# The transforms over D split nine by 64, with the nine points on VectorE

## The chip, the cores and the metric

The kernel runs on one core of a Trainium2 chip. The metric is the time on the device in microseconds (us), the median of the runs shown. Each core has a matrix engine (TensorE, PE in the profile), VectorE (DVE), ScalarE (ACT), GpSimd (POOL) and a queue engine for transfers (SyncE, SP), which run side by side and wait for one another through semaphores. Matmuls write to PSUM, which has eight banks per partition; the other engines evacuate PSUM to SBUF.

## The reference

The output is `g * a + (1 - g) * b`, for x of 2048 rows (S) and 576 columns (D):

```
X = rfft2(x);  X = X * (w_r + 1j * w_i);  a = irfft2(X, s=(S, D))
b = (gelu(x2 @ w_gate) * (x2 @ w_up)) @ w_down        # F = 4608
g = sigmoid((x * gate_w).sum(-1))
```

What is computed is the output and the gradients for all inputs but the second x (x2): for x, w_r, w_i, the three weight matrices and gate_w. So the spectral part needs the 2-D transform of x and of the gated gradient, their products with the filter and with one another (the gradient of the filter has the shape of the filter, 2048 by 289), and two inverse transforms: of the filtered spectrum and of the spectrum that gives the gradient for x.

## The kernel before, in words

The kernel has two phases. In the first, 18 groups g of 256 columns of F are taken with four blocks m of 512 rows each: 72 rows of work, each some 12 to 15 us long. In one of them TensorE does z (L466, L471: the gradient times w_down, transposed), xy (L475, L482: x2 times gate and up), and weight-gradient jobs of the group before: dwd (L595), dw (L613), and in the block m = 2 a tail dwt (L627). ScalarE evacuates xy and z (L494 to L504), computes sigmoids (L530 to L534), and VectorE does the products of GELU and its gradient (`H_ew1`, `H_ew2`; L509 to L551). The stores of weight gradients go out on POOL's queue (L605, L620, L631, L632).

The spectral work ("fft units") is fitted into these rows in slots. `want(pr)` says how many units are done by row pr, from the list `FIRST` for the first nine rows and from a linear share after it. The first slot of a row (`k0`) lies inside the second xy; the others lie between the weight-gradient jobs. All units and z share one PSUM tile of two banks: `pz` has one buffer, so the next z or unit waits until the evacuation of the unit before it.

The forward units work on 16 tiles t of 128 rows for x and 16 for the gradient. The transform over D = 576 is split as 6 residues r (column = 6 q + r) by 96: ScalarE first copies a row tile to `xq` with stride 6 (`sort`, L728; L730 with a scale for the gradient), `u1` multiplies each residue (a lhsT of 96 columns) with a table Rt over the rows (L657, six matmuls of 128 columns), evacuates to Z, and `u2` multiplies Z with the table F (L671, six of 98 columns). ScalarE evacuates to `ve` (L677) and VectorE combines the six points (L679 to L698) into the spectrum `Vt` in natural order of l = 0 to 288, which is stored to DRAM (`scr_x`, `scr_g`).

The middle units take p = 0 to 7, each with 16 of the rows g of the spectrum: `prefetch(p)` loads Vp and the filter Wt (twelve transfers on POOL, L770), `s2` (L779) finishes the transform over S in the units x0, x1, g0, g1 (evacuated at L784), `products` puts the products with the filter in a list `side`, which VectorE works off after `H_ew1`, and `s1` (L857) begins the inverse transforms in four units. The gradient of the filter, `o1`, is stored directly. `prefetch(0)` stands ahead of the middle units, `prefetch(1)` in the last x/g unit of p = 0, and `prefetch(p + 2)` in the second `s1` of p.

The second phase (from some 912 us) accumulates the two matmul results over F per tile of 128 rows (L1235) and, between them, finishes the inverse transforms over D: for each tile i and each w in (output, gradient) `fold` (VectorE, L1266 on) makes F from the spectrum, `z_piece` (L1287, six matmuls of 128 columns) and `d_piece` (L1297, six of 96) transform it, and ScalarE evacuates the six residues to `yo` with stride 6 (L1299). `x_out` (L1415) evacuates the accumulators; `post` mixes with the gate.

The order of the work is written out by hand; nothing reorders it later. Each engine runs its instructions in the order of the program.

Of the kernel before, what the change touches and what calls it, by code (L numbers as in the profile page):

```python
# [38 lines left out]
LQ = 49  # L39
SIN60 = math.sqrt(0.75)  # L40

# [20 lines left out]
def iotas(nc, res, unit):  # L62
    tb = Tables()
    G, V = nc.gpsimd, nc.vector
    kw = dict(allow_small_or_imprecise_dtypes=True)
    tb.halfpi = res.tile([P, 1], F32, name="halfpi")
    V.memset(tb.halfpi[:], math.pi / 2)
    tb.pi = res.tile([P, 1], F32, name="pi")
    V.memset(tb.pi[:], math.pi * EPS_SCALE)
    tb.warm = res.tile([P, 1], F32, name="warm")  # L70
    nc.scalar.activation(tb.warm[:], tb.halfpi[:], ACT.Sigmoid)
    tb.lrow = unit([LQ], F32, name="lrow")
    G.iota(tb.lrow[:], pattern=[[1, LQ]], base=0, channel_multiplier=0, **kw)
    tb.dcol = res.tile([P, 6], F32, name="dcol")
    for k, (r, step, n) in enumerate(((1, 1, 2), (0, 0, 1), (5, -1, 3))):
        k0 = (0, 2, 3)[k]
        G.iota(tb.dcol[:, k0:k0 + n], pattern=[[step, n]], base=r, channel_multiplier=6, **kw)
    tb.late = []
    tb.Rt = []
    return tb  # L80
# [39 lines left out]
def build_F(nc, tb, unit):  # L120

    V = nc.vector
    step = 2.0 * math.pi / D
    X = unit([6, LQ], F32, name="XF")
    y = unit([6, LQ], F32, name="yF")
    V.tensor_tensor(X[:], tb.dcol[:].unsqueeze(2).to_broadcast([P, 6, LQ]), tb.lrow[:].unsqueeze(1).to_broadcast([P, 6, LQ]), op=ALU.mult)
    V.tensor_scalar(y[:], X[:], 1.0 / D, MAGIC, op0=ALU.mult, op1=ALU.add)
    V.tensor_scalar(y[:], y[:], -MAGIC, -float(D), op0=ALU.add, op1=ALU.mult)
    V.tensor_tensor(X[:], X[:], y[:], op=ALU.add)
    V.scalar_tensor_tensor(y[:], X[:], -1.0, X[:], op0=ALU.mult, op1=ALU.max)  # L130
    tb.F = unit([6, 2, LQ], name="Ft")

    def sines():
        nc.scalar.activation(tb.F[:, :, 0], y[:], ACT.Sin, bias=tb.halfpi[:], scale=-step)
        nc.scalar.activation(tb.F[:, :, 1], X[:], ACT.Sin, scale=-step * EPS_SCALE)
    tb.late.append(sines)


def build_I(nc, tb, ftile, small, out):

    V = nc.vector
    R = slice(0, 2 * LQ)
    col = small([8])
    lp, ge, mul, add, e0, e1, half, q_ = (col[R, k:k + 1] for k in range(8))
    X, y = ftile()[R], ftile()[R]

# [5 lines left out]
    kw = dict(allow_small_or_imprecise_dtypes=True)  # L152
    nc.gpsimd.iota(q_, pattern=[[0, 1]], base=0, channel_multiplier=1, **kw)
    nc.gpsimd.iota(X.rearrange("p (r q) -> p r q", r=6), pattern=[[1, 6], [6, 96]], base=0, channel_multiplier=0, **kw)
    V.tensor_scalar(ge, q_, float(LQ), None, op0=ALU.is_ge)
    ts(lp, ge, -float(LQ), 0.0)
    tt(lp, lp, q_, ALU.add)
    ts(mul, ge, -2.0, 1.0)
    tt(mul, mul, lp, ALU.mult)
    ts(add, ge, -float(D // 4), float(D // 4))  # L160
    ts(X, X, mul, add)
    ts(y, X, 1.0 / D, MAGIC)
    ts(y, y, -MAGIC, -float(D), op0=ALU.add, op1=ALU.mult)
    tt(X, X, y, ALU.add)
    V.tensor_scalar(e0, lp, 0.0, None, op0=ALU.is_equal)
    V.tensor_scalar(e1, lp, float(LQ - 1), None, op0=ALU.is_equal)
    tt(half, e0, e1, ALU.add)
    ts(half, half, -0.5, 1.0)
    o = out[R].rearrange("p r q -> p (r q)")
    nc.scalar.activation(o, X, ACT.Sin, scale=2.0 * math.pi / D * EPS_SCALE)  # L170
    V.tensor_scalar(o, o, half, None, op0=ALU.mult)
# [120 lines left out]
def kernel(  # L292
# [355 lines left out]
    def fwd_units(src, dst, scale):  # L648
        zs = {}
        CLS = (1, 2, 0, 5, 4, 3)  # L650

        def u1(t):
            def f():
                zps = pftile()
                row = src.pop(t)
                for k, r in enumerate(CLS):
                    nc.tensor.matmul(zps[0:96, k // 3, k % 3 * P:(k % 3 + 1) * P], lhsT=row[:, r], rhs=tb.Rt[t], start=True, stop=True)  # L657
                zs[t] = unit([2, 3 * P], name="Z")
                if scale is None:
                    nc.scalar.copy(zs[t][0:96], zps[0:96, :, 0:3 * P])  # L660
                else:
                    nc.scalar.activation(zs[t][0:96], zps[0:96, :, 0:3 * P], ACT.Copy, scale=scale)
            return f

        def u2(t):
            def f():
                Z = zs.pop(t)
                vps = pftile()
                w = 2 * LQ
                for k in range(6):  # L670
                    nc.tensor.matmul(vps[:, k // 3, k % 3 * w:(k % 3 + 1) * w], lhsT=Z[0:96, k // 3, k % 3 * P:(k % 3 + 1) * P],  # L671
                                     rhs=tb.F[0:96, k].rearrange("p c l -> p (c l)"), start=True, stop=True)
                Vt = half([2, DF], name="Vt")
                ve = unit([2, 3, 2, LQ], F32, name="ve")
                sd = unit([2, 3, 2, LQ], F32, name="sd")
                M = unit([6, 2, LQ], F32, name="vm")
                nc.scalar.copy(ve[:].rearrange("p b k c l -> p b (k c l)"), vps[:, :, 0:3 * w])  # L677
                lo, hi = ve[:, 0], ve[:, 1]
                V.tensor_tensor(sd[:, 0], lo, hi, op=ALU.add)  # L679
                V.tensor_tensor(sd[:, 1, :, 0], hi[:, :, 0], lo[:, :, 0], op=ALU.subtract)  # L680
                V.tensor_tensor(sd[:, 1, :, 1], lo[:, :, 1], hi[:, :, 1], op=ALU.subtract)
                e, o = sd[:, 0, 2], sd[:, 1, 2]
                for k, op in enumerate((ALU.add, ALU.subtract)):
                    V.tensor_tensor(M[:, k], sd[:, 0, 0], sd[:, 0, 1], op=op)
                    V.tensor_tensor(M[:, 4 + k, 1::-1], sd[:, 1, 0], sd[:, 1, 1], op=op)
                p_, m_ = M[:, 0], M[:, 1]
                for c, op in enumerate((ALU.subtract, ALU.add)):
                    V.scalar_tensor_tensor(M[:, 2, c], m_[:, c], 0.5, o[:, c], op0=ALU.mult, op1=op)
                V.scalar_tensor_tensor(M[:, 3], p_, -0.5, e, op0=ALU.mult, op1=ALU.add)
                up = Vt[:, :, 96:DF - 1].rearrange("p c (j l) -> p j c l", j=2)[:, :, :, 0:LQ]  # L690
                dn = Vt[:, :, 1:193].rearrange("p c (j l) -> p j c l", j=2)[:, :, :, 94:47:-1]
                V.tensor_tensor(Vt[:, :, 0:LQ], e, p_, op=ALU.add)
                V.scalar_tensor_tensor(Vt[:, 0, DF - 1:DF - LQ:-1], o[:, 0, 0:LQ - 1], -1.0, m_[:, 0, 0:LQ - 1], op0=ALU.mult, op1=ALU.subtract)
                V.tensor_tensor(Vt[:, 1, DF - 1:DF - LQ:-1], m_[:, 1, 0:LQ - 1], o[:, 1, 0:LQ - 1], op=ALU.subtract)
                for c in range(2):
                    V.scalar_tensor_tensor(up[:, :, c], M[:, 4:6, c], SIN60, M[:, 2:4, c], op0=ALU.mult, op1=ALU.add)
                for c, s_, op in ((0, -SIN60, ALU.add), (1, SIN60, ALU.subtract)):
# [786 lines left out]
```

## Time and profile before

| | |
|---|---|
| Median of 3 runs | 1360.02 us (1359.3 to 1360.67) |
| The profiled execution | 1359.78 us, its span 1358.0 us |
| Granted TensorE clock | 1.0 |
| TensorE busy | 1343.7 us (99%) |
| VectorE busy | 879.8 us (65%) |
| ScalarE busy | 770.3 us (57%) |
| POOL busy | 243.9 us (18%) |
| Chain that ended last | PE 98% |

The span is the time from the first to the last instruction in the trace; some 1.8 us lie around it. Busy times of an engine add the times in which it works; its instructions overlap in their pipelines, so the time from start to start of two dependent instructions is shorter than the duration of one. The chain that ended last is followed back from the last instruction, at each step to what released it; a share of 98% says that nearly the whole span is TensorE at work, one matmul after another. In groups, "idle before" is the time that the engine stood idle just before these instructions, with what ended it.

### The profile page before, as it was taken

How to read it: one execution, taken by the hardware profiler on the slowest of the kernel's cores; microseconds unless marked ns; L12 is line 12 of the kernel's file. 1: busy time of each engine (PE TensorE's matmuls, PEld its weight loads, DVE VectorE, ACT ScalarE, POOL GpSimd, SP SyncE). 2: the span in 40 equal slices, each digit the busy share in tenths (PEclk: the TensorE clock that was granted, in tenths of full speed). 3: DMA queues.
4: the chain of work that ended last, by engine and by line, in shares of the span. 5: the costliest groups of instructions: out<-in, count | busy, mean ns of one | idle time of the engine just before them, and what ended most of it. 6: DMA issues, size and time to landing. Idle time of an engine off the chain costs nothing.

```text
span 1358.0 us, 26951 instructions
## 1 busy us (share of the span) xinstructions
PE 1343.7 (99%) x10279; PEld 900.6 (66%) x10360; DVE 879.8 (65%) x2353; ACT 770.3 (57%) x1380; POOL 243.9 (18%) x488
## 2 busy tenths in 40 slices
PE   9999999999999999999999999999999999999999
PEld 6556656656655655655655655568888888888887
DVE  7988898898857876876776855526543455354420
ACT  6797887888767776776777675622332232232210
POOL 3011111111313633434323311000000000000000
PEclk9999999999999999999999999999999999999999
DMA  9624435534543644644754658499999787888773
GB/s 224 181 73 125 137 100 150 155 99 132 152 138 108 180 119 119 168 123 118 175 141 116 159 127 181 116 240 237 201 205 213 162 175 160 167 163 175 155 154 75
DMA packets 493606, 207.05 MB, mean 152 GB/s; under 512 B 313346, under 2 KB 485444, under 8 KB 493476
## 3 DMA queue, kind: packets, MB, share of 16 engines
q1 hardware_dynamic: 467330, 170.47, 55.2%
q0 software_dynamic: 15040, 24.38, 6.4%
q10 hardware_dynamic: 11106, 10.48, 3.1%
q8 instruction: 81, 1.33, 0.4%
q14 instruction: 49, 0.40, 0.1%
HBM read 41.18 MB, written 89.11 MB: 96 GB/s over the span
## 4 chain that ended last, share of the span: by engine, by line
PE 98%; issue 1%; DMA 1%; SPq 0%; ACT 0%; DVE 0%
PE acc L1235 31%; PE wps L613 18%; PE xy L482 18%; PE wps L595 10%; PE z L466 9%; PE wps L627 2%; PE xy L475 2%; PE z L471 2%; PE pf L657 1%; PE acc L1287 1%; PE pf L671 1%; PE acc L1297 1%; PE pf L857 1%; PE pf L779 1%; DMA xn<-in_A_x_dram 1%
## 5 line engine op out<-in xcount | busy, mean ns | idle before, releaser
L1235 PEld LDWEIGHTS <-pin 128*128 128x128 bf16 x3456 | 334.9, 98 | 82.4
L482 PE MATMUL xy<-wgu,xT 128*128 128x512 bf16 x1082 | 257.6, 379 | 8.6 <-issue 7.3
L613 PE MATMUL wps<-dH,xn 128*128 128x512 bf16 x1141 | 263.7, 379 | 0.6
L613 PEld LDWEIGHTS <-xn 128*128 128x128 bf16 x1152 | 111.3, 98 | 125.4 <-issue 0.6
L482 PEld LDWEIGHTS <-xT 128*128 128x128 bf16 x1152 | 105.7, 98 | 132.9 <-issue 24.8
L595 PE MATMUL wps<-dB,A 128*128 128x288 bf16 x1152 | 149.9, 286 | 0.0
L620 POOL DMA_DIRECT2D out_dram<-dw x134 | 73.1, 549 | 423.5 <-ACT dw L564 411.7
L1235 PE MATMUL acc<-wgT,pin 128*128 128x288 bf16 x1152 | 146.5, 286 | 0.0
L1235 PE MATMUL acc<-wd_all,pin 128*128 128x288 bf16 x1152 | 146.4, 286 | 0.0
L1235 PE MATMUL acc<-wuT,pin 128*128 128x288 bf16 x1152 | 146.0, 286 | 0.0
L1299 ACT ACTIVATE yo<-acc 128x288 bf16<-128x288 f32 x64 | 67.4, 1246 | 132.1 <-PE acc L1297 120.7
L466 PE MATMUL z<-wdT,dOT 128*128 128x256 bf16 x1152 | 138.2, 273 | 0.1
L595 PEld LDWEIGHTS <-A 128*128 128x128 bf16 x1152 | 111.8, 98 | 32.9
L494 ACT ACTIVATE da<-z,omg 128x256 bf16<-128x256 f32 x288 | 111.9, 470 | 28.8 <-PE z L471 28.6
L466 PEld LDWEIGHTS <-dOT 128*128 128x128 bf16 x1152 | 112.0, 98 | 22.3 <-ACT dOT L438 0.5
L1415 DVE TENSOR_TENSOR b16t<-acc,f32t 128x288 bf16<-128x288 f32 x32 | 14.6, 457 | 168.4 <-PE acc L1235 168.3
L503 ACT CAST xb<-xy 128x512 bf16<-128x512 f32 x144 | 85.5, 594 | 39.5 <-PE xy L482 39.5
L1289 ACT CAST Z<-acc 98x384 bf16<-98x384 f32 x64 | 27.5, 481 | 112.8 <-PE acc L1287 112.8
L504 ACT CAST hu<-xy 128x512 bf16<-128x512 f32 x144 | 87.8, 610 | 0.0
L541 DVE TENSOR_TENSOR xb<-xb,sg 128x1024 bf16<-128x1024 bf16 x48 | 33.1, 689 | 81.2 <-ACT sg L533 81.2
L501 ACT ACTIVATE q<-xy 128x512 bf16<-128x512 f32 x144 | 80.6, 605 | 3.6 <-PE xy L482 3.6
L564 ACT CAST dw<-wps 128x512 bf16<-128x512 f32 x72 | 42.2, 588 | 60.1 <-PE wps L613 45.8
(518 smaller groups left out, 1803.0 us busy)
## 6 DMA issues: line engine op xcount, KB each, us to landing
scr<-dH SPq DMA_DIRECT2D x144, 256.0 KB, 3.4
scr<-A SPq DMA_DIRECT2D x72, 256.0 KB, 2.4
out_dram<-dw POOLq DMA_DIRECT2D x134, 64.0 KB, 1.9
wd_all<-in_B_w_down_dram SPq DMA_DIRECT2D x3, 1728.0 KB, 12.8
out_dram<-dwd POOLq DMA_DIRECT2D x34, 144.0 KB, 2.6
scr_p<-Vt SPq DMA_DIRECT2D x32, 144.5 KB, 2.9
Vp<-scr_p ACTq DMA_DIRECT2D x32, 144.5 KB, 4.1
wgu<-in_B_w_gate_dram SPq DMA_DIRECT2D x18, 256.0 KB, 4.5
```

Source lines behind the costliest of these rows:

```text
L466: nc.tensor.matmul(zo(t), lhsT=dOT[:, ci, t, :], rhs=wdT[:, ci, :], start=(t % 4 < 2 and ci == 0), stop=False)
L482: nc.tensor.matmul(xy[k][:, t % 2, :], lhsT=xT[:, ci, t, :], rhs=wgu[:, ci, :], start=False, stop=(ci == 3))
L494: nc.scalar.activation(da[:, t, :], z[:, t % 2, t // 2, :], ACT.Copy, scale=omg32[:, 4 * m + t:4 * m + t + 1])
L501: nc.scalar.activation(q[:, h, :], xy[:, :, 0:FG], ACT.Square)
L503: nc.scalar.copy(xb[:, h, :], xy[:, :, 0:FG])
L504: nc.scalar.copy(hu[:, h, :], xy[:, :, FG:2 * FG])
L564: wcopy[0](out, in_)
L595: nc.tensor.matmul(wps[:, :288], lhsT=tl(0, t)[:, fch * P:(fch + 1) * P], rhs=dB[:, t, h * 288:(h + 1) * 288], start=(t == 0), stop=(t == ...
L613: nc.tensor.matmul(wps[:].rearrange("p a b -> p (a b)"), lhsT=xn[:, t, c * P:(c + 1) * P], rhs=kt[t // 4][1][:, t % 4].rearrange("p k f -> ...
L620: wst[0].dma_start(ov[:, c, fsl], dw[:, k, :])
L1235: nc.tensor.matmul(acc[:, :288], lhsT=src[:, r, :], rhs=w_of(r)[:, h * 288:(h + 1) * 288], start=(first and r == 0), stop=(last and r == F ...
L1299: nc.scalar.activation(yv[:, 3 * b:3 * b + 3], ps[:, 0:288].rearrange("p (r q) -> p r q", r=3), ACT.Copy, scale=(SD2, 1.0)[w])
```

## The change

The transform over D is split as 9 by 64 in place of 6 by 96, and the nine-point part moves to the other side of the matmuls, in f32 on VectorE.

In the forward part, `sort` no longer copies with a stride. For a pair of tiles t it runs `nine_a` (the cosine side, 14 operations) with the first and `nine_b` (the sine side, 10 operations) with the second, on nine contiguous runs of 64 columns (column = 64 j + r). The gradient's rows are scaled first, in place, both tiles in one go. The results have 64 + 4 x 128 columns: class 0, and four classes with a cosine and a sine half. `u1` has five matmuls and two evacuations, `u2` four matmuls of 128 columns and one of 66, and ScalarE evacuates directly to `Vt`; VectorE's combination is gone. `Vt` now holds l by classes: the 33 values l = 0, 9, ..., 288 first, then eight blocks of 32.

Since the spectrum is by classes, the filter must be too: in the unit x0 of each p, ScalarE copies Wt to a new tile Wp (a read with stride 9, 1,152 elements, and one of four elements), ahead of the matmuls' evacuation; and `out_dw` copies the filter's gradient back to natural order on VectorE before it is stored.

In the second phase `fold` is three copies, `z_piece` has five matmuls, `d_piece` four of 128 columns and one of 64, evacuated in f32 to R; and with w = 1 `nine` (27 VectorE operations for both w) makes the two `yo`. The tables F and It are built for the new split: more iotas on POOL at the start, more VectorE operations in `build_I`. `FIRST` is now nine zeros (it ended in 1, 3), and `sort_ahead` runs the sorts one ahead of what the next row needs.

```
-    FIRST = (0, 0, 0, 0, 0, 0, 0, 1, 3)
+    FIRST = (0,) * 9
...
 def u1(t):
-                for k, r in enumerate(CLS):
-                    nc.tensor.matmul(zps[0:96, k // 3, k % 3 * P:(k % 3 + 1) * P], lhsT=row[:, r], rhs=tb.Rt[t], start=True, stop=True)
-                zs[t] = unit([2, 3 * P], name="Z")
+                for k in (1, 2, 3, 4, 0):
+                    c0 = 128 * k - (64 if k else 0)
+                    nc.tensor.matmul(zps[:, int(k == 0), max(k - 1, 0) * P:max(k, 1) * P], lhsT=row[:, c0:c0 + P], rhs=tb.Rt[t], start=True, stop=True)
+                Z = zs[t] = unit([5 * P], name="Z")
+                for b, c in enumerate((slice(0, 4 * P), slice(4 * P, 5 * P))):
+                    if scale is None:
+                        nc.scalar.copy(Z[:, c], zps[:, b, 0:c.stop - c.start])
...
 def u2(t):
+                o = vps[:, 0].rearrange("p (c o q) -> p c o q", c=2, o=8)
+                for k in range(1, 5):
+                    nc.tensor.matmul(o[:, :, k - 1:9 - k:9 - 2 * k, :], lhsT=Z[:, (k - 1) * P:k * P],
+                                     rhs=tb.F[:, (k - 1) * P:k * P].rearrange("p (c h q) -> p c h q", c=2, h=2), start=True, stop=True)
+                nc.tensor.matmul(vps[:, 1, 0:66], lhsT=Z[:, 4 * P:5 * P], rhs=tb.F[:, 512:578], start=True, stop=True)
                 Vt = half([2, DF], name="Vt")
+                nc.scalar.copy(Vt[:, :, 33:DF], vps[:, 0].rearrange("p (c l) -> p c l", c=2))
+                nc.scalar.copy(Vt[:, :, 0:33], vps[:, 1, 0:66].rearrange("p (c q) -> p c q", c=2))
...
+    def nine_a(q, x, d):
+        V.tensor_tensor(Y[:], x[:, 1:8:3], x[:, 8:1:-3], op=ALU.add)
+        V.tensor_tensor(s3, x[:, 3], x[:, 6], op=ALU.add)
+        V.tensor_tensor(e, x[:, 0], s3, op=ALU.add)
+        V.scalar_tensor_tensor(m, s3, -0.5, x[:, 0], op0=ALU.mult, op1=ALU.add)
+        V.tensor_tensor(W[:, 0:2], Y[:, 0:2], Y[:, 1:3], op=ALU.subtract)
...
+    def nine_b(q, x, d):
+        V.tensor_tensor(Y[:], x[:, 1:8:3], x[:, 8:1:-3], op=ALU.subtract)
+        V.tensor_tensor(sm[:, 0], x[:, 3], x[:, 6], op=ALU.subtract)
...
 def sort(dst, t):
-            nc.scalar.copy(xq[t], xn[:, t, :].rearrange("p (q r) -> p r q", r=6))
+                if dst is gq:
+                    nc.scalar.activation(graw[k][:, j], graw[k][:, j], ACT.Copy, scale=g32[:, 2 * k + j:2 * k + j + 1])
+        x = xn[:, 2 * k:2 * k + 2, :] if dst is xq else graw[k][:]
+        (nine_a, nine_b)[h](q[:, :, 0:64], x.rearrange("p t (j r) -> p j t r", j=9),
+                            q[:, :, 64:D].rearrange("p t (k v r) -> p k t v r", k=4, v=2))
...
 def s2(p, which, j):
+                if which == "x" and j == 0:
+                    w, wp = st[p, "w"], unit([2, 2, DF], name="Wp")
+                    nc.scalar.copy(classes(wp)[:, :, 1:DF].rearrange("p k (o q) -> p k o q", o=9),
+                                   classes(w)[:, :, 0:DF - 1].rearrange("p k (q o) -> p k o q", o=9))
+                    nc.scalar.copy(classes(wp)[:, :, 0:1], classes(w)[:, :, DF - 1:DF])
+                    st[p, "w"] = wp
...
 def out_dw():
-                o = st[p, "o1"]
+                o1, o = st[p, "o1"], unit([2, 2, DF], name="dwt")
+                V.tensor_copy(classes(o)[:, :, 0:DF - 1].rearrange("p k (q o) -> p k q o", o=9),
+                              classes(o1)[:, :, 1:DF].rearrange("p k (o q) -> p k q o", o=9))
+                V.tensor_copy(classes(o)[:, :, DF - 1:DF], classes(o1)[:, :, 0:1])
...
-                (0.0, out_dw),
+                (1.6, out_dw),
...
+    sorts = [u.sort for u in slots if hasattr(u, "sort")]
 def sort_ahead(pr):
-        due = [u.sort for u in slots[sorted_to[0]:to] if hasattr(u, "sort")]
+        need = sum(1 for u in slots[:to] if hasattr(u, "sort"))
+        need += need % 2
+        to = max(need, min(sorted_to[0] + 1, need + 1, len(sorts)) if pr > 6 else 0)
+        due = sorts[sorted_to[0]:to]
...
 def fold(i, w):
+            F = ft[i, w] = sp.tile([P, 578], BF16, tag="F", name="F", bufs=2)
+            V.tensor_copy(Fm[:, 0], vm[:, 0:4])
+            V.tensor_copy(Fm[:, 1], vm[:, 7:3:-1])
+            V.tensor_copy(F[:, 512:578].rearrange("p (c q) -> p c q", c=2), v[:, :, 0:33])
...
 def z_piece(i, w):
+            for k in range(4):
+                nc.tensor.matmul(ps[0][:, k * P:(k + 1) * P], lhsT=F[:, k * P:(k + 1) * P], rhs=RT[:, i, :], start=True, stop=True)
+            nc.tensor.matmul(ps[1][0:66, 0:P], lhsT=F[:, 512:578], rhs=RT[:, i, :], start=True, stop=True)
...
 def d_piece(i, w):
+            for k in range(4):
+                nc.tensor.matmul(ps[0][:, k * P:(k + 1) * P], lhsT=Z[:, k * P:(k + 1) * P], rhs=It[:, 64 + k * P:64 + (k + 1) * P],
+                                 start=True, stop=True)
+            nc.tensor.matmul(ps[1][:, 0:64], lhsT=Z[0:66, 4 * P:5 * P], rhs=It[0:66, 0:64], start=True, stop=True)
+            nc.scalar.activation(R[:, 1:9, w, :].rearrange("p (v k) r -> p k v r", v=2), ps[0][:].rearrange("p (k v r) -> p k v r", k=4, v=2), ACT.Copy, scale=sc)
+            nc.scalar.activation(R[:, 0, w, :], ps[1][:, 0:64], ACT.Copy, scale=sc)
+            if w == 1:
+                nine(i)
```

## The prediction

> **What bounds the kernel now.** I read the page's busy times first, then the chain of work that ended last:
>
> ```profile
> PE 1343.7 (99%) x10279; PEld 900.6 (66%) x10360; DVE 879.8 (65%) x2353; ACT 770.3 (57%) x1380; POOL 243.9 (18%) x488
> PE 98%; issue 1%; DMA 1%; SPq 0%; ACT 0%; DVE 0%
> ```
>
> TensorE is the chain; nothing else ends last for more than 1% of the span. So every PE nanosecond that goes is gained, every wait of PE is lost, and work on the other engines is free while PE does not wait for it. The view of PE's waits lists 7.3 us of "issue" in pieces of at most 0.2 us, and two single waits of 1.1 and 0.5 us. Before the change there is nothing else to win from waits.
>
> Next the page's groups and the chain in a window, for the price of the pieces the change touches:
>
> ```profile
> 180.82 0.34 PE pf L657 x6
> 183.75 0.27 PE pf L671 x6
> 1000.62 0.34 PE acc L1287 x6
> 1011.58 0.26 PE acc L1297 x6
> L728 ACT COPY xq<-xn 128x576 bf16<-128x576 bf16 x16 | 16.1, 1008 | 0.0
> L1299 ACT ACTIVATE yo<-acc 128x288 bf16<-128x288 f32 x64 | 67.4, 1246 | 132.1 <-PE acc L1297 120.7
> ```
>
> First number start, second duration in the chain; in the groups busy time, mean ns, idle before. A 128-column matmul costs PE 0.34/6 = 56 ns, a 98-column one 45, a 96-column one 44.
>
> Then the slack of VectorE and ScalarE by stretch. In 180 to 230 us PE is busy 49.52 of 50, DVE 43.32, ACT 40.78; in 420 to 470 us DVE 45.76 and ACT 35.92; in 1000 to 1050 us DVE 16.56, ACT 13.38.
>
> Last, the place where the change makes the chain depend on something new: the load of the filter on POOL, and ACT and PE just behind it (timelines; start, duration).
>
> ```profile
> 412.08 0.54 POOL L605 DMA_DIRECT2D out_dram<-dwd  x1 [8.53 <-DMA scr<-dH]
> 412.70 3.04 POOL L770 DMA_DIRECT2D Wt<-in_A_w_r_dram  x6
> 415.73 3.02 POOL L770 DMA_DIRECT2D Wt<-in_A_w_i_dram  x6
> 418.74 0.57 POOL L605 DMA_DIRECT2D out_dram<-dwd  x1
> ...
> 419.94 0.37 ACT L564 CAST dwt<-wps 128x256 bf16<-128x256 f32 x1 [0.47 <-PE wps L627]
> 424.84 0.60 ACT L504 CAST hu<-xy 128x512 bf16<-128x512 f32 x1
> 426.57 1.28 ACT L784 CAST Xx<-pf 64x578 bf16<-64x578 f32 x2 [1.14 <-PE pf L779]
> ...
> 426.13 0.41 PE L779 MATMUL pf<-Vp,Btab 128*128 128x289 bf16 x2
> 428.96 1.91 PE L466 MATMUL z<-wdT,dOT 128*128 128x256 bf16 x16
> ```
>
> Today Wt of p=1 (twelve transfers of 0.507 us issue) is read first by VectorE's products at 450.19, long after it lands.
>
> **The change, part by part.** The sum is made against the profiled execution, 1359.78 us (span 1358.0 and 1.78 around it); the median of the three runs, 1360.02, stands 0.24 above it.
>
> *PE work.* u1 and the z pieces go from six 128-column matmuls to five: 32 x 56 ns each = 1.8 + 1.8 us. u2: 6 x 45 = 0.27 becomes 4 x 56 + one of 66 columns (about 30 to 45) = 0.25 to 0.27; d pieces 0.26 becomes 0.25 to 0.27: together 0 to 0.8. All of it lies on the chain: -3.6 to -4.4, I take -4.0.
>
> *VectorE, forward.* u2's recombination goes: 3.0 us from its first start (194.41) to the next work (197.41), per t. nine_a and nine_b come, for two t: 24 f32 operations. Starts of f32 operations there stand 0.17 apart for 98 elements, 0.22 for 147, 0.38 for 294; so 0.20 for 128, 0.34 for 256, 0.48 for 384: nine_a 2 x 0.48 + 0.34 + 11 x 0.20 = 3.5, nine_b 0.96 + 0.34 + 7 x 0.20 = 2.7, 6.2 per pair of t against 6.0. Sixteen pairs: +3 us on an engine with 6.7 of 50 us free. They hang on data that is long there, run one slot row ahead, and stand before H_ew1; what they can do is make H_ew1's sigmoid chain late. H_ew2's products (L541) wait 81.2 us in all for the sigmoid, so VectorE usually stands ahead. Ripple 0 to 4 us; I take 0.5, nearer zero, because by the order on the engine every sort is finished before its u1. If that cover goes, the price is the 0.3 to 0.5 us by which a 3.5-us block is late, in each of 16 rows.
>
> *ScalarE, forward.* The x sort (16 x 1.0) and the sorting scale of g (16 x 1.1) go; 16 plain scales (about 0.81, L1000's mean for the same shape) come. Evacuations in two pieces: +0.1 each on waits with 0.6 to 1.1 us of margin. Taken as 0; bounds -0.5 and +1, the margin being the cover.
>
> *Middle, the reordered filter.* Each p gets, in its first x slot and ahead of the Xx evacuation, an ACT copy of 2 x 2 x 288 elements read with stride 9. The L728 row reads 576 elements with stride 6 in 1.008 us; doubling the part per element gives 1.74 to 1.85, and 0.2 for the four leftover elements: 2.0. Bounds 1.24 (an unstrided row, 1,024 elements in 1.06, scaled) and 2.4.
>
> Most important is p=1. The FIRST list now starts at zero slots, so that work runs one slot later, and prefetch(1) is issued behind POOL's two dwd stores and two dwt stores, which wait for the dwt evacuation (ends 420.31): stores to about 421.4, then Wt to 427.5, landed near 430.4 (median 3.0 to 3.5 us for w_i, at least 1.8). x0 of p=1 now has the second slot, at 426.13. ACT reaches the copy at 425.4 and stands until 430.4; copy to 432.4, both evacuations to 433.7. The z matmuls due at 428.96 need the same PSUM tile (pool pz, one buffer): PE loses 433.7 - 429.0 = 4.7 us. Bounds: 3.0 (fast landing, cheap copy) and 7.2 (the longest landing seen, 5.6). Queued behind the blocked copy on ACT are Xx, dw and s; all wait with it, but PE is stopped already. The other p load ten or more us ahead (p=3's issue ends at 498.8, its use is at 521.9), so they pay the copy alone. p=4 has x0 and x1 only 8 matmuls (1.73 us) apart: 2.0 + 1.28 against about 2.0, so 1.4 (0.2 to 1.8). Three with x0 in the slot inside xy: 0.2 each, 0.6 (0 to 1.2). The rest have cover of some 0.4 us.
>
> The Trainium skill, "DMA: Bandwidth & Descriptors", section "Anatomy of one DMA — SWDGE (gpsimd) path", fits about 2.0 us plus bytes/436e3 to one DMA, 2.04 us for Wt's 18.1 KB; with it the p=1 stall would be 3.3 us and the total 1.4 lower, but this trace's median is 1.9 to 3.5 us, and I keep the trace.
>
> The same skill's "VectorE: DVE Perf Modes", section "The TRN2 errata — SBUF-src ops pay a fixed extra latency per instruction", gives ScalarE 224 cycles plus one per element at 1.2 GHz, an estimated 0.67 us for L728's 576 elements where the trace shows 1.008; it has no term for the stride, and by it the copy would be 1.15 and each stall 0.7 shorter.
>
> *out_dw's copy* (VectorE, about 1.4 us per p): no PE wait hangs on it but through the side-work list; 0, up to 1 in the 420 to 470 stretch, where VectorE has 4.2 of 50 us free.
>
> *Start.* Longer POOL iotas (+0.75) and build_F delay VectorE's first copy; x lands at 9.2 us anyway: 0.2 (0 to 0.6).
>
> *Phase 2.* ACT loses the strided yo (64 x 1.25 us) and gains two plain evacuations. VectorE swaps two folds of 2.75 us per tile for three copies each (about 0.9) and nine (27 operations, about 6.4): +2.7 per tile of some 18 us, in a stretch where it is a third to half busy. x_out can stand behind nine and the post work (10.4 us) in late tiles; the banks it frees are next used about a tile later. I take 0; bounds 0 and 2 us on each of the last four tiles. The tail has 30 us between VectorE's last gradient input and its use.
>
> Sum: -4.0 + 0.5 + 4.7 + 1.4 + 0.6 + 0.2 = +3.4: 1359.8 + 3.4 = 1363.2 in the profiled execution, 1363.4 on the median.
>
> **Rivals.**
> - *Faster: p=1's wait is hidden.* If Wt(1) has landed by about 425.4, or the copy has a later slot, 4.7 falls away: -4.0 + 0.5 + 1.4 + 0.6 + 0.2 = -1.3; if the copies of the other p are covered too, -4.0: 1356 to 1358.5. For it: PE saving is certain, the queue order is the only reason for the wait. Against: the dwt stores do stand ahead of it on POOL, and their evacuation cannot be earlier than the tail matmuls. It decides when the landing is earlier than 426.5.
> - *Half a wait*, 1 to 3 us: 1359 to 1361.5, no measurable change.
> - *Slower still: VectorE's blocks tell.* nine_a of 3.5 us in a row of 12.4, with 6.8 us of H_ew1 and H_ew2 in it, holds the sigmoid 0.3 to 0.5 us in each of 16 rows: +5 to +8, or late tiles of phase 2 wait 1 to 2 us each for x_out: 1367 to 1373. For it: 87% in the forward stage. Against: the average slack of 6.7 per 50 us and the 81 us of waiting at L541. It decides where a 128-element f32 operation takes over 0.25 us from start to start.
>
> **How the numbers follow.** Forecast with p=1's stall (1361.5 to 1366.5) 0.45; faster 0.25; half a wait 0.12; slower still 0.18. A measurement of this kernel tells 0.2%, 2.7 us, from no change: same is 1357.3 to 1362.7. Of the forecast's 0.45 about 0.08 lies under 1362.7, so same 0.20, slower 0.37 + 0.18 = 0.55, faster 0.25. The range from 1355.8 (best bound of the PE saving, all waits hidden) to 1370.5 leaves out about a tenth on each side; the likeliest case's own range is 1361.5 to 1366.5.
>
> **What would show it.** In the profile after: PE about 4 us less busy; one PE z wait of 3 to 7 us near 430 us, released by ACT's evacuation, and ACT idle before the filter copy with a Wt transfer as releaser; that copy near 1.8 us; nine_a near 3.5 us; no new PE waits in 80 to 370 us or after 930. I am wrong if Wt(1) lands before its copy, if PE waits recur in every forward row, or if z or pf matmuls of 128 columns cost other than 56 ns.

## The result, and the profile after

The changed kernel takes 1375.81 us (median of 4 runs, 1373.67 to 1377.29) against 1360.13 us: 1.0115 times as long, with a 95% interval of 1.0097 to 1.0132, or 15.7 us. The forecast was 1363.4 us with a range up to 1370.5. The profiled execution took 1375.93 us, its span is 1374.2 us, 16.2 more than before. The page's busy times and the chain that ended last:

```profile
PE 1344.5 (98%) x10151; PEld 896.4 (65%) x10232; DVE 930.8 (68%) x2227; ACT 726.2 (53%) x1446; POOL 245.0 (18%) x492
PE 84%; DVE 7%; ACT 4%; issue 3%; DMA 1%; POOL 1%; DVEq 0%; ACTq 0%; POOLq 0%
```

TensorE has 128 matmuls fewer, as the diff says, and is still most of the chain. But VectorE and ScalarE now make up 11% of it. The view of TensorE's waits (us in total, times, longest) says where:

```profile
PE z L505 <- ACT Xx L845: 5.9, 2, 4.0
PE pf L696 <- ACT da L533: 3.3, 1, 3.3
PE z L505 <- ACT xb L542: 1.8, 1, 1.8
PE pf L840 <- ACT Xx L845: 1.6, 1, 1.6
PE wps L634 <- DVE A L579: 1.2, 1, 1.2
PE pf L711 <- ACT Z L702: 0.9, 1, 0.9
```

Before, no line of this view but the first matmul's was above half a microsecond, apart from the 7.3 us in 46 tiny gaps, which the changed kernel has too. The wait of 1.8 us is z of row 4, at 42.11 us. The view names ScalarE's xb, which ended just before; in five of the runs below it names the transfer of w_down for the wait at this place, and so does the table below. The list does not say what a wait costs in the end, so I compared the start of each row's first z matmul (72 rows, numbered from 0) in the two traces. The table shows the steps of that difference, in us:

| Place | Step | What stands there |
|---|---|---|
| rows 0 to 6 | +1.7 | z of row 4 waits for w_down of the next group |
| rows 8 and 9 | +5.7 | the first nine-point blocks |
| row 21 | +1.2 | a fourth unit; two scalings of the gradient on ScalarE |
| rows 10 to 28, the rest | -2.0 | smaller matmul count, 0.07 to 0.16 per row |
| rows 7 and 29 to 30 | +0.2 | units moved by the new FIRST (-0.33, +0.52) |
| p = 0 | +1.85 | the copy of the filter |
| p = 1 | +4.2 and +1.6 | wait for the filter's load and copy; the row behind it |
| p = 4 | +2.0 | the copy, with x1 close behind x0 |
| p = 5, 6, 7 | +1.1 | the copy, 0.37 to 0.39 each |
| second phase | -1.6 | smaller matmul count |

The table's rows sum to 16.0 (each is the difference of the two traces' row lengths, added up over its place); a few steps of 0.04 make up the 16.15 of the spans.

The place that the prediction named first, p = 1 (timelines of POOL, ScalarE and TensorE; start, duration, in brackets the idle time before and what ended it):

```profile
429.31 0.55 POOL L670 DMA_DIRECT2D out_dram<-dwt  x1 [3.81 <-ACT dwt L603]
430.46 3.02 POOL L822 DMA_DIRECT2D Wt<-in_A_w_r_dram  x6
433.47 3.12 POOL L822 DMA_DIRECT2D Wt<-in_A_w_i_dram  x6
...
438.21 2.29 ACT L832 COPY Wp<-Wt 128x1152 bf16<-128x1152 bf16 x1 [3.91 <-DMA Wt<-in_A_w_i_dram]
440.50 1.28 ACT L845 CAST Xx<-pf 64x578 bf16<-64x578 f32 x2
...
441.84 3.05 PE L505 MATMUL z<-wdT,dOT 128*128 128x256 bf16 x16 [4.00 <-ACT Xx L845]
```

POOL's queue reaches the filter only behind the dwt stores, ScalarE stands 3.91 us for the load, copies for 2.29 (and 0.11 for the four elements), evacuates, and TensorE stands 4.0 us ahead of z. The last line shows something more: sixteen z matmuls take 3.05 us where they took 1.91 before.

The place to which the sum of the prediction gave 0.5 us, from the chain (start, duration, what):

```profile
99.39 0.69 DVE dH L590
100.08 0.47 DVE nY L753
...
102.44 0.69 DVE xq L761 x3
103.14 0.35 DVE s L548
...
103.58 0.70 DVE s L549
...
104.30 1.07 ACT sg L572
...
105.39 1.06 ACT s L573
106.45 1.46 ACT da L533 x4
...
107.95 0.69 PE pf L696 x5
```

VectorE ends H_ew2 of one row at 100.08, does `nine_b` until 103.14, and only then the first operations of `H_ew1`. The sigmoid on ScalarE waits for these, and `da`, the evacuation of z, stands behind the sigmoid in ScalarE's queue. All units share z's PSUM tile, so u1 in the first slot starts when da has ended. TensorE stood from 104.67 to 107.95. Here too the matmuls behind it are slow (u1's five take 0.69 us instead of 0.28). The granted clock, in windows of both places (columns: window, length, then busy time with counts of PE, weight loads, DVE, ACT, POOL, then PEclk, DMA share, GB/s):

```profile
104.50:107.90 3.40, 0.17 (x1) 0.00 (x0) 3.08 (x6) 3.37 (x7) 0.00 (x0) 1.00 0.60 152
107.90:111.30 3.40, 3.35 (x14) 1.81 (x14) 3.33 (x9) 3.03 (x7) 0.00 (x0) 0.50 0.19 41
111.30:114.70 3.40, 3.40 (x33) 2.74 (x31) 3.19 (x13) 1.71 (x5) 0.54 (x1) 1.00 0.03 9
439.00:442.40 3.40, 0.56 (x6) 0.50 (x6) 1.23 (x2) 3.36 (x6) 0.00 (x0) 1.00 0.00 0
442.40:445.80 3.40, 3.40 (x21) 1.88 (x18) 2.35 (x5) 1.28 (x2) 1.11 (x2) 0.50 0.12 39
```

Behind each of the two long waits the clock is 0.50 for 3.41 us, in which TensorE is busy nearly throughout: 1.7 us of work lost on top of the wait. Of the 5.7 us at rows 8 and 9, 1.7 are this, 3.3 the wait itself and 0.8 what is left of a wait of 1.2 in row 8.

### The profile page after: what moved, and what is told of

It is laid out like the page before. It is cut to its first block, busy times and chain, and to the rows that moved or that the text cites. A ratio compares the mean times of both kernels' runs of the same rounds, so it can differ in the third digit from the quotient of the medians.

```text
span 1374.2 us, 26754 instructions
## 1 busy us (share of the span) xinstructions
PE 1344.5 (98%) x10151; PEld 896.4 (65%) x10232; DVE 930.8 (68%) x2227; ACT 726.2 (53%) x1446; POOL 245.0 (18%) x492
## 4 chain that ended last, share of the span: by engine, by line
PE 84%; DVE 7%; ACT 4%; issue 3%; DMA 1%; POOL 1%; DVEq 0%; ACTq 0%; POOLq 0%
PE acc L1302 29%; PE wps L652 15%; PE xy L521 15%; PE wps L634 8%; PE z L505 8%; PE xy L514 2%; PE wps L666 2%; PE z L510 1%; ACT Wp L832 1%; POOL out_dram L901 1%; PE pf L696 1%; PE acc L1341 1%; PE acc L1350 1%; DVE sn L887 1%; PE pf L840 0%
## 5 line engine op out<-in xcount | busy, mean ns | idle before, releaser
L1354 ACT ACTIVATE nR<-acc 128x512 f32<-128x512 f32 x32 | 19.1, 597 | 150.2 <-PE acc L1352 77.6
L1343 ACT CAST Z<-acc 128x512 bf16<-128x512 f32 x32 | 18.7, 585 | 125.3 <-PE acc L1342 121.0
```

## The experiments

Theory A: all of the loss comes from single waits at the places of the table, each with its own cause, and the half clock behind the long ones is their consequence. Rival B: VectorE, busier by 51 us, has become a bound, and a wait taken away comes back elsewhere. Of each kernel the median is given, and the ratio to the kernel before, run on the same chip; steps and waits are those of its profiled execution.

### The filter's copy in the side list

```
 def s2(p, which, j):
-                if which == "x" and j == 0:
-                    ... nc.scalar.copy(Wp <- Wt by classes)
 def products(p):
-            X, G, W = st[p, "x"], st[p, "g"], st[p, "w"]
+            X, G, w = st[p, "x"], st[p, "g"], st[p, "w"]
+            W = unit([2, 2, DF], name="Wp")
+            def by_classes():
+                V.tensor_copy(classes(W)[:, :, 1:DF].rearrange("p k (o q) -> p k o q", o=9),
+                              classes(w)[:, :, 0:DF - 1].rearrange("p k (q o) -> p k o q", o=9))
+                V.tensor_copy(classes(W)[:, :, 0:1], classes(w)[:, :, DF - 1:DF])
+                (1.5, by_classes),
                 (0.8, mul("m1", X, W[:, 0])),
```

> The filter's copy to classes leaves ScalarE and the first x slot of each p; VectorE does it as the first piece of the side list, about 1.3 us per p, when all transfers have long landed. Theory A (TensorE loses the time in single waits behind the ScalarE copy): the trace of the changed kernel has TensorE fall back by 1.85 us in p=0, 4.2 in p=1 with 1.6 more in the row behind it, 2.1 in p=4 and 3 x 0.38 later, 10.9 in all; all of it goes: 1376 - 11 = about 1365, the waits of z and pf for Xx are gone and only one stretch at half clock is left. Rival B (VectorE is overloaded in the middle stage, so that work put on it comes back as waits): at most half of that, 1370 or more.

Measured: 1364.17 us, ratio 1.0031 (1.0019 to 1.0042); 11.6 us less than the changed kernel, where 10.9 were expected. The steps at p = 0, 1, 5, 6 and 7 are gone (p = 0 becomes -0.25), p = 4 keeps 0.42, and 0.29 is new two rows behind p = 1. In the profiled execution 1.3 of the gain is the start's, which differs from one execution to the next (below). No wait for Xx is left (L951 is the first matmul's):

```profile
PE pf L696 <- ACT da L533: 3.3, 1, 3.3
PE wps L634 <- DVE A L579: 1.2, 1, 1.2
PE pf L951 <- DVE halfpi L70: 1.1, 1, 1.1
PE pf L711 <- ACT Z L702: 0.9, 1, 0.9
```

One stretch at half clock is left, the one near 108 us. VectorE does the copy in 1.23 us at 432.06, where ScalarE needed 2.29. Rival B falls for the middle stage: VectorE has more work there and TensorE waits for none of it.

### The filter of p = 1 loaded earlier

```
 def s2: if which == "g" and j == 1:
-                    if p == 0:
-                        prefetch(p + 1)
 def first():
             prefetch(0)
+            prefetch(1)
```

> The changed kernel with one edit: the filter of p=1 is loaded directly behind that of p=0, some 45 us earlier; the ScalarE copy stays in the first x slot. Theory A (two separate costs: the copy itself, and for p=1 the wait for its late load): p=1 then pays the copy alone, about 1 us in place of 4.2 + 1.6 at half clock, while p=0, p=4 and the three later ones still pay their 1.85, 2.0 and 3 x 0.38: 1376 - 5 = about 1371. Rival C (the load is not what p=1 waits for; the copy on ScalarE is): unchanged, 1375 to 1376.

Measured: 1371.36 us, ratio 1.0082 (1.0067 to 1.0097). At p = 1 the steps are 0.18 and, two rows later, 0.72 us in place of 4.2 and 1.6; p = 0, 4, 5, 6 and 7 keep 1.86, 2.00 and 3 x 0.37. The wait in row 9, 3.30 us here, comes 1.2 us dearer in this run: the clock is 0.50 for 6.83 us behind it, not for 3.41. So the two costs are separate: the late load is what p = 1 paid for, the copy is what all the others pay for.

### The block behind H_ew1

```
 def sort_ahead(pr):
-        for q in due[:1]:
-            sort(*q)
-        return due[1:]
+        return due
...
                 state += [*H_ew1(g, tiles, da), da]
+                for q in unsorted[:1]:
+                    sort(*q)
+                unsorted = unsorted[1:]
```

> The first nine-point block of a row stands behind H_ew1 on VectorE instead of ahead of it; nothing else is changed. Theory A (the block makes H_ew1 late, its sigmoid late, and with it ScalarE's evacuation of z, on which the next use of the same PSUM tile waits): the 5.7 us near 100 us and the 1.2 us near 265 us go: 1376 - 7 = about 1369, and the half clock behind the first is gone. Rival B (VectorE is simply full in the forward stage, 46 to 48 of 50 us): the lateness moves to H_ew2 and the forward stage stays within 2 us of where it was, about 1374 to 1376.

Measured: 1374.73 us, ratio 1.0106 (1.0089 to 1.0123): 1.1 us gained, not 7. In the trace the step of 5.7 at rows 8 and 9 is down to 0.98, and the half clock there is gone, as theory A has it. The 1.2 of row 21 stay, against the expectation. And new steps of 0.2 to 0.67 stand in rows 13, 18 to 20, 23, 24 and 27, and p = 1 costs 0.8 more, since the clock is 0.50 for 6.83 us behind its wait of 3.96. ScalarE's timeline in row 23 shows what is new:

```profile
289.04 1.49 ACT L778 ACTIVATE graw<-graw,g 128x576 bf16<-128x576 bf16 x2
290.38 0.62 ACT L603 CAST dw<-wps 128x512 bf16<-128x512 f32 x1
290.85 0.65 ACT L715 CAST Vt<-pf 128x512 bf16<-128x512 f32 x1
```

The edit also moved the two scalings of the gradient, from behind da to just ahead of the evacuations that free u2's PSUM. So the run decides nothing about rival B; the version "The block between" below repeats it without that side effect.

### The tables of F later

```
-    ...                                      # the iotas of F, at the start
-    build_F(nc, tb, unit)                    # at the start
                 elif m == 1:                 # second row of group 0
                     next(makeB)
+                    iotas_F(nc, res, tb, unit)           # the same iotas
+                    build_F(nc, tb, unit)
```

> POOL's new iotas and the build of the table F are moved from the start to the second row, so that POOL's loads of the weight tails are issued first, as before the change. Theory A (the longer start on POOL pushes the transfers behind it, and the transposing load of w_down for the second group lands 1.8 us later): the 1.8 us that TensorE waits at 42 us go: about 1374. Rival B (that load is late for another reason, by chance or by the queue of SyncE alone): the wait stays and the time is unchanged within 0.5 us.

Measured: 1376.53 us, ratio 1.0120 (1.0105 to 1.0135). No gain; theory A fell here. The step ahead of the z of row 4 was 0.01 in this run, but 0.98 came one row before: VectorE now builds the tables there, from 28.9 to 31.8 us, and its copy of dOT, for which TensorE waits 0.6, stands behind them at 33.8. And the wait for w_down does not need the change: with the same start the step of row 4 was 1.88 in the changed kernel, 0.55 in the first experiment, 1.64 in the second and 0.11 in the third, and in a run of the kernel before (the eight-copy control below) it was 1.37. It differs from one execution to the next; why, no run here tells.

### All three

The three edits above together.

> All three edits together. Theory A: the gains add, 11 + 7 + 1.8 = about 19.5 us, and the time is 1356 to 1357, below the kernel before, because TensorE's own saving of about 3.9 us is left. Rival B (VectorE's load is the cause): less than two thirds of it, 1363 or more, since all three edits leave VectorE's work as it is or raise it.

Measured: 1364.43 us, ratio 1.0038 (1.0024 to 1.0053), no better than the first edit alone. The expectation was wrong by the two edits that had brought nothing: the new small waits of the moved scaling and the tables' work ate what the rows 8 and 9 gave back.

### The block between, the scaling where it was

On top of the side list; the sort is cut in two.

```
 def sort_ahead(pr):
+        if due:
+            scaled(*due[0])          # the two ScalarE scalings, behind da as before
+        return due
...
                 state += [*H_ew1(g, tiles, da), da]
+                for q in unsorted[:1]:
+                    sort(*q)             # nine_a or nine_b on VectorE
```

> On top of the side-list edit (1364.2): the first nine-point block of a row stands between H_ew1 and H_ew2, and the scaling of the gradient's rows stays on ScalarE where it was, behind z's evacuation (the earlier run had moved it as well, and small waits of 0.67 us came at the rows with it). Theory A (position of the block, not its length): the 5.7 us near 100 us shrink to about 1, no 0.67 us waits, forward stage 4.5 us better: about 1359.5. Rival B (VectorE is full, the lateness comes back elsewhere): 1362.5 or more.

Measured: 1359.43 us, ratio 0.9995 (0.9986 to 1.0005), as expected. Rows 8 and 9 cost 0.99, no stretch at half clock is left, and row 21 is down from 1.2 to 0.58. Row 13 keeps its step of 0.43. Moving the same work to another place on the same engine was worth 4.7 us: rival B falls for the forward stage.

### The scaling at the row's end

```
                 flush()
+                for q in sorts[sorted_to[0]:sorted_to[0] + 2]:
+                    if q[1] // 2 in graw:
+                        scaled(*q)
```

> As the run before, and the two scaling operations of a pair (1.45 us) go to the end of the row before, where ScalarE waits for VectorE. Theory A: the 1.2 us at row 22 (265 us) go too, and no row of the gradient's half loses time: about 1358.3, faster than the kernel before. Rival B: no gain over the run before.

Measured: 1362.33 us, ratio 1.0019 (1.0010 to 1.0029), 2.9 us worse (1.7 between the two profiled executions). The step at row 21 stays 0.59, so the place of the scaling is not its cause, and rows 17, 20, 24 and 25 show steps of 0.12 to 0.44 where the run before had -0.07 to -0.15: the scalings now stand ahead of the sigmoid, and da behind it. ScalarE's waiting for VectorE at the row's end was not free time, since its next work is what TensorE waits for.

What is left of row 21 can be read in the run before. The kernel before has three units in this row, u1 twice and u2 once; the new one has four, each twice. One u1 is 0.28 us of matmuls, and u2 now comes only eight matmuls behind the u1 whose evacuation it needs (TensorE and ScalarE):

```profile
259.91 0.44 PE L696 MATMUL pf<-Rt,xq 128*128 128x128 bf16 x5
260.19 1.14 PE L634 MATMUL wps<-dB,A 128*128 128x288 bf16 x8
260.67 0.88 ACT L702 ACTIVATE Z<-pf 128x512 bf16<-128x512 f32 x2
261.59 0.38 PE L711 MATMUL pf<-Ft,Z 128*128 128x128 bf16 x4 [0.26 <-ACT Z L702]
```

In the changed kernel that last wait is 0.87. The two together are most of what is left.

### Two rows later

```
-    FIRST = (0,) * 9
+    FIRST = (0,) * 11
-        to = max(need, min(sorted_to[0] + 1, need + 1, len(sorts)) if pr > 6 else 0)
+        to = max(need, min(sorted_to[0] + 1, need + 1, len(sorts)) if pr > 8 else 0)
```

First with the block ahead of `H_ew1`, as the change has it (and the copy in the side list):

> The side-list version (1364.2) with the block ahead of H_ew1, as the change has it, but the first units start two rows later (eleven zeros in FIRST, sorts from row 9 on). Theory A' (the 5.7 us near 100 us come because VectorE is still behind from the tables and scalings that it does in rows 4 to 8, and the first blocks fall on it there): with two rows to catch up, most of the 5.7 us go and the half clock with them: about 1359 to 1360. Rival B' (any first block ahead of H_ew1 does it): the loss moves two rows down, 1364 again.

Measured: 1357.78 us, ratio 0.9982 (0.9973 to 0.9992). No loss is left at rows 8 to 11, the clock is 1.0 throughout. So the place in the row was not the cause by itself; the first blocks also fell on rows in which VectorE was still behind. The windows of the kernel before show one part of that (columns as above, DVE is the third):

```profile
50.00:75.00 25.00, 24.79 (x190) 15.99 (x191) 24.34 (x55) 19.86 (x38) 4.46 (x7) 1.00 0.51 143
75.00:100.00 25.00, 24.68 (x172) 14.49 (x174) 20.60 (x51) 24.26 (x43) 2.71 (x5) 1.00 0.20 61
```

From 50 to 75 us VectorE was busy 24.34 of 25 already, with H_ew1, H_ew2, the tables and the scalings. The other part is ScalarE, which computes the sines of the tables next. In the changed kernel (ScalarE, then VectorE):

```profile
75.58 1.28 ACT L152 ACT_TABLE_LOAD   x1
82.72 1.06 ACT L569 ACTIVATE s<-s 128x1024 bf16<-128x1024 bf16 x1
81.44 0.43 DVE L323 TENSOR_TENSOR Btab<-oB,msB 128x256 bf16<-128x256 f32 x1 [3.44 <-ACT oB L320]
83.81 0.69 DVE L580 TENSOR_TENSOR xb<-xb,s 128x1024 bf16<-128x1024 bf16 x1 [1.94 <-ACT s L569]
92.73 0.42 DVE L548 TENSOR_SCALAR s<-q 128x1024 bf16<-128x1024 bf16 x1
```

From 75.58 on ScalarE is at the tables, the sigmoid comes at 82.72, and VectorE stands idle for the two, 3.44 and 1.94 us (0.96 and 1.94 before the change): it is not full here, it waits. H_ew2 then ends at 88.8, and the first block of 4.0 us puts the next H_ew1 to 92.73; in the kernel before it started at 86.23. Of these 6.5 us 4.0 are the block, 1.7 come from the start, and 0.8 are the longer sines of F (1.6 us in place of 0.8). The second block, of 3.1, follows one row later. With the start two rows later VectorE waits for the tables in the same way (2.15 and 1.94 us), but no block stands behind it. No run separates VectorE's full rows from ScalarE's sines. Before the change, ScalarE did the first sorts, and no block stood there.

Then with the block between:

> The version with the block between H_ew1 and H_ew2 (1359.4), started two rows later in the same way. Theory A': the 1.0 us left at rows 8 to 9 goes, the row of 13 may lose as much since the slots stand closer: 1358.5, a little below the kernel before. Rival B': 1359.4 or more, no difference.

Measured: 1357.44 us, ratio 0.9979 (0.9970 to 0.9988), 2.8 us faster than the kernel before. From the version with the block ahead it differs by 0.3 us, which the two intervals do not tell apart: once the start is later, no gain from the block's place is shown. Its waits, apart from the 46 small gaps, are the start's, the first matmul's (L959) and two of less than 0.5:

```profile
PE z L505 <- DMA wdT<-in_B_w_down_dram: 1.2, 1, 1.2
PE pf L959 <- DVE halfpi L70: 1.1, 1, 1.1
PE fx L987 <- ACT xT L988: 0.4, 1, 0.4
PE pf L696 <- ACT Z L702: 0.3, 1, 0.3
```

A control, the kernel before with its first units two rows later:

```
-    FIRST = (0, 0, 0, 0, 0, 0, 0, 1, 3)
+    FIRST = (0, 0, 0, 0, 0, 0, 0, 0, 0, 1, 3)
 def sort_ahead(pr):
-        n = int(pr != 7)
+        n = int(pr != 9)
```

> A control for the two versions that start later: the kernel before with its first units two rows later (FIRST ends in 1, 3 after nine zeros), nothing else. Theory A' (what the versions gain over the kernel before is the smaller number of matmuls, 3.5 to 4 us, and the later start only keeps VectorE's new blocks off the busy rows; TensorE waits for nothing there before the change): 1360.1, within 1 us. Rival (the later start is itself worth something): 1358.5 or less.

Measured: 1360.80 us, ratio 1.0005 (0.9995 to 1.0015). Starting later is worth nothing by itself. That what the two versions gain is the smaller number of matmuls is argued, not separated by a run: 2.4 and 2.8 us, where the rows without a wait and the second phase of the changed kernel give 3.6.

### What a standstill costs in clock

The kernel before, with idle copies on ScalarE at one place (a single run of each):

```
 def s2(p, which, j):
+                if p == 1 and which == "x" and j == 1:
+                    z = unit([2, 2, DF], name="held")
+                    for _ in range(5):          # or 8
+                        nc.scalar.copy(z[:], st[p, "w"][:])
```

> The kernel before, with five copies of 1,156 elements on ScalarE (some 1.2 us each) put once ahead of the evacuation of x1 of p=1; the copies are used by nothing. TensorE has 1.1 us of cover there, so it stands still for about 4.8 us, once. Theory D (a standstill of this length also costs clock: after the two long waits of the changed kernel the granted clock is 0.5 for 3.41 us): the time rises by 4.8 + 1.7 = 6.5 us, to 1366.5, and the clock shows one stretch of 3.4 or 6.8 us at 0.5. Rival: 4.8 us alone, clock 1.0 throughout, 1365.

Measured: 1363.6 us. z is 3.6 us late (not 4.8: less was uncovered than I had worked out), the time rises by as much, and the clock stays at 1.0. Theory D as I had put it, that the length of the wait decides, falls: 3.28 us cost clock at 108 us, 3.6 do not here. What differs is how the wait lies. In windows of 3.41 us, counted from the point at which the record of the granted clock begins in this execution (columns as above):

```profile
427.40:430.80 3.40, 1.90 (x9) 0.78 (x8) 3.31 (x8) 3.31 (x4) 0.00 (x0) 1.00 0.00 0
430.80:434.20 3.40, 1.45 (x14) 1.30 (x14) 0.75 (x2) 3.35 (x5) 0.60 (x2) 1.00 0.02 5
```

The wait straddles an edge, and TensorE is busy for a good part of either window.

> The kernel before with eight idle copies in place of five (which gave 3.6 us of standstill and no loss of clock): TensorE stands still for about 7.1 us. Theory D' (the clock is judged in fixed windows of 3.41 us, and it halves for a window behind one in which TensorE hardly works; 3.6 us that straddle a boundary do nothing): 7.1 us must cover a whole window, so one or two windows at 0.5 appear and the time rises by 7.1 + 1.7 or 3.4: 1368.9 to 1370.6. Rival (the clock fell in the changed kernel for another reason): 1367.2 and clock 1.0.

Measured: 1369.54 us. z is 7.2 us late and the row behind it another 1.7:

```profile
430.40:433.80 3.40, 0.00 (x0) 0.00 (x0) 1.86 (x3) 3.31 (x4) 0.00 (x0) 1.00 0.00 0
433.80:437.20 3.40, 0.18 (x2) 0.11 (x2) 0.00 (x0) 3.32 (x5) 0.00 (x0) 0.50 0.00 0
437.20:440.60 3.40, 3.40 (x18) 2.18 (x18) 1.96 (x4) 1.34 (x2) 1.11 (x2) 0.50 0.15 43
```

A whole window without a matmul, and the clock is 0.50 until TensorE has worked through one. In the changed kernel the window ahead of each slow stretch holds 0.17 and 0.56 us of matmuls in 3.40, so it need not be empty. The two runs with 6.83 us at half clock show the same from the other side. In windows of the second experiment, laid in the same way:

```profile
103.23:106.64 3.41, 1.08 (x6) 0.39 (x4) 3.09 (x6) 2.66 (x4) 0.00 (x0) 1.00 0.68 189
106.64:110.05 3.41, 2.44 (x11) 1.25 (x11) 3.38 (x6) 3.04 (x9) 0.00 (x0) 0.50 0.38 77
110.05:113.47 3.42, 3.42 (x16) 2.19 (x15) 3.28 (x13) 1.56 (x3) 0.00 (x0) 0.50 0.00 0
```

The wait is that of the changed kernel, 3.30 us, but it lies across an edge, two windows at half clock follow, and 2.9 us of work are lost in place of 1.7. In the traces of all the runs here, divided into such windows, every window at full clock with at most 1.16 us of matmuls was followed by half clock, and none with 1.45 or more.

The Trainium skill, "TensorE: Matmul & The Clock Gate", section "Part 1: The HAM clock gate (the "warmup" mystery)", says the same: activity is judged in free-running windows of 3413 ns, an idle one halves the clock and a busy one restores it. The records here have that length (3.413 us, or twice that), and the four cases agree; but a window that counts as idle held up to 1.16 us of matmuls. So the cost of a wait of some 3.3 us and more depends on where it falls. The spread of the changed kernel's four runs over 3.6 us is not explained by it: all four have a mean granted clock of 0.998, hence much the same time at half clock.

## Why the prediction was wrong

The sum of the forecast was +3.4 us; measured are +15.7, above the stated range and above the 1367 to 1373 of the rival "slower still" too. The main step that failed is the ripple of VectorE's blocks in the forward stage, put at 0.5 us and measured at 5.7. The copy in the other p (2.0) was too small by 3.0, and half clock had no term at all (3.3, of which 1.7 are in the 5.7). Term by term:

- **PE work, -4.0 (-4.4 to -3.6).** Right, at the small end: -2.0 in the forward rows and -1.6 in the second phase, and 56 ns per matmul held.
- **The wait at p = 1, 4.7 (3.0 to 7.2).** Right in mechanism: 4.2, and 1.6 of half clock behind it. That the size came so near is partly luck: the last transfer landed 1.9 us after its issue where some 3.4 had been taken from the median of all p (in the kernel before, the loads of p = 1 itself had landed in 1.8 to 2.1), and the copy with its four elements took 2.4, not 2.0. The queue order on POOL, the landing, ScalarE and the shared PSUM tile did what was written. The rival "faster" (the wait is hidden) is out.
- **VectorE in the forward stage, ripple 0.5 (0 to 4).** This is the step that failed: 5.7 us, of which 1.7 are half clock; the other 4.0 are the upper bound of the term. The blocks were sized at 3.5 and 2.7 us and took 4.0 and 3.1, because an operation that reads the one just before it starts 0.31 to 0.33 behind it, not 0.20; with durations of 0.28 and 0.29, that is longer than the one operation takes, not shorter as the text on the profile before has it. That alone was not the fault. I took the slack from a window at 180 to 230 us, 6.7 of 50, and put it to the rows at 75 to 105, where the trace of before had 0.7 of 25 just ahead of them, and where VectorE then stands waiting for ScalarE's sines. And I priced a late block at its own 0.3 to 0.5 us, where a whole block of 3 to 4 us is late when VectorE arrives late. The rival "slower still" has the right mechanism, H_ew1's sigmoid, but spread over 16 rows; it happened in two, and its test (a 128-element operation above 0.25 us from start to start) was not what decided: dependent ones were above it, the others not.
- **Nothing for the clock.** The forecast had no term for it. Two waits of 3.3 and 4.0 us each cost 1.6 to 1.7 more, 3.3 us in all (already counted in the rows 8 and 9 and behind p = 1).
- **The copy in the other p, 2.0 together.** Under-sized, with 5.0: p = 0 paid 1.85 where I had put it among "the rest" with cover, because I had looked only at whether its load was early. Its slot has 16 matmuls of dwd, some 2 us, between it and the next z; with a copy of 2.4 and evacuations of 1.3 us that cannot do. p = 4 paid 2.0 (1.4 taken, 1.8 the bound), the three later ones 1.1 (0.6). The copy took 2.29 + 0.11 us, near the upper bound of 2.4 instead of the middle.
- **ScalarE, forward, 0 (-0.5 to 1).** Row 21 lost 1.2; 0.6 of it goes with the block's place, most of the rest is the row's fourth unit and u2's wait for Z, a cover that the forecast had put at 0.6 to 1.1 us.
- **Start, 0.2.** The profiled execution shows +1.7, but executions differ there by as much, before the change too; the 0.2 is neither shown nor refuted. The longer sines of F on ScalarE at 77 us (0.8 us) were not in the sum.
- **Second phase, VectorE's 2.7 us more per tile at no cost.** Right: no wait came, the phase is 1.6 us shorter.

## What to carry to other kernels

Slack is a matter of the stretch: before work is moved to an engine, its busy share has to be read in the very rows where the first of it falls, above all behind a start that leaves the engine late. A copy put ahead of a PSUM evacuation must be held against the time until TensorE needs that PSUM in every place where it occurs, not only in the one where its input is late. The same change was worth -2.8 us or +15.7 by where the filter's copy and the blocks stand and in which row the first units begin, so the place of each added operation is part of the design.

## What the runs showed of the hardware

The granted clock made a wait dearer than its length: 3.28 and 4.0 us of standstill cost 1.6 to 1.7 us more each in the changed kernel, and 7.2 us cost 1.7 more in the control; the same two waits cost 2.9 and 2.6 more in the runs in which they lay across an edge of the 3.41-us windows with too few matmuls ahead of it (1.08 and 1.01 us). A wait of 3.6 us that left 1.90 and 1.45 us of matmuls in its two windows, and all of the waits of 2 us or less, cost only themselves. An operation on 128 f32 elements on VectorE started 0.20 us behind the one before, or 0.31 to 0.33 behind it when it read its result. A bf16 copy of 1,152 elements read with stride 9 took 2.29 us on ScalarE and 1.23 us on VectorE.
